# First query and key loads merged, and fourteen more zero products on TensorE, at the start of a cosine-attention and hard-swish kernel

## The chip, the cores and the metric

The kernel runs on one core of a Trainium2 chip. The metric is the device time of one launch in microseconds (us), smaller is better. Each kernel is run several times and the median counts.

## The reference, cut to what matters

Inputs are q, k and v of 8 batches, 12 heads, 448 positions and 64 numbers each, in float32, and two weight matrices of 768x2048 and 2048x768.

```python
q_n = q / (np.linalg.norm(q, axis=-1, keepdims=True) + 1e-06)
k_n = k / (np.linalg.norm(k, axis=-1, keepdims=True) + 1e-06)
scores = np.matmul(q_n, k_n.transpose(0, 1, 3, 2)) / tau
...
attn = np.exp(scores)
attn = attn / (np.sum(attn, axis=-1, keepdims=True) + 1e-09)
...
h = x @ w_in
relu6 = np.clip(h + 3.0, 0.0, 6.0)
g = h * relu6 / 6.0
return (g @ w_out).astype(np.float32)
```

Here x is the attention output with the heads of a position side by side: 3584 rows of 768.

## The kernel before, in words

The whole program is one list of short commands, the table `PLAN` (line 19). A command such as `SQ.2.a.0.7` calls one function with its arguments; each function issues instructions to one or more engines. An engine carries out its own instructions strictly in the order of the list, so the list fixes each engine's order, and semaphores fix who waits for whom. A last letter names the engine: v is DVE (VectorE), a is ACT (ScalarE), p is POOL (GpSimd).

Work goes in 48 pairs of heads (six pairs per batch). Queries and keys are loaded, squared and normalised in items of four heads: item 0 holds queries, item 1 the keys that belong to them, item 2 queries again, and so on through 48 items. An item is a tile of 128 partitions x 2 halves x 448 numbers, 448 KB. The commands around the change are:

- `LQ.j` (line 254): loads item j, one DMA issued by SP. `LQ.0.0` and `LQ.0.1` load the first and the second half of item 0 alone, 224 KB each. `LV` loads values, `W` weights.
- `SQ.j.e.c.n` (line 283): squares n of the item's groups of 64 columns, from c, on engine e. For items 0 and 1 the 14 groups of both halves are counted through, so 0 to 6 are the first half.
- `RE.j` (line 300): DVE sums the squares; `RE.0.0` one half alone.
- `NO.d` (line 318): four small ACT operations (lines 326 to 329) that make the inverse norms of items 2d and 2d+1; `NO.0.0` and `NO.0.1` make those of item 0 and of item 1 alone.
- `NM.j` (line 333): multiplies the item by its inverse norms, on DVE or POOL.
- `TR.j` (line 393): seven TensorE transposes of item j into a PSUM bank; `CQ` (ACT or DVE) and `CK` (DVE) copy queries and keys of a pair of heads from it to SBUF.
- `SC.i.g` (line 474): scores of pair i, group g, on TensorE; `EX.i.g` (line 508): their exponentials on ACT; `VA.i.g` (line 529): the products with the values on TensorE; `FI.i` (line 548): DVE divides by the sums.
- `DP.n` (line 1139): n zero products on TensorE. Each multiplies a 128x128 block of zeros with 248 columns of zeros and writes columns of the PSUM tile PV that nobody reads. Nothing waits for them; they only keep TensorE at work while it would wait.

TensorE's part at the start is, in its order: 23 zero products, the transposes of item 0, 10 zero products, the transposes of item 1, four score products (`SC.0.0`, `SC.0.1`), 3 zero products, two score products (`SC.0.2`), two small ones (`SC.0.3`), the transposes of item 2, the scores of pair 1, 2 zero products, and then the first products with values. A score product of pair 0 goes to one of two PSUM tiles that ACT empties with `EX`, so `SC.0.2` waits for `EX.0.0` and `SC.0.3` for `EX.0.1`.

After the start the list weaves attention, the first matrix product (line 671) and the second one (line 837) together, and TensorE has hardly a pause in them.

Of the kernel before, what the change touches and what calls it, by code (L numbers as in the profile page):

```python
# [16 lines left out]

FIRST = 18
PLAN = [
    "LQ.0.0 LQ.0.1 SQ.0.v.6.2 SQ.0.a.0.6 RE.0.0 SQ.0.a.8.6 RE.0.1 LQ.1.0 SQ.1.p.0.4 SQ.1.a.4.3 RE.1.0 LQ.1.1 SQ.1.v.11.3 SQ.1.a.7.4 RE.1.1 LQ.2 NO.0.0",  # L20
    "SQ.2.a.0.7 LQ.3 NM.0.v.0 NM.0.v.1 NO.0.1 DP.23 TR.0.Z RE.2 LQ.4 LQ.5 NM.1.p.0 NM.1.p.1 SQ.3.a.0.7 RE.3 SQ.5.p.0.7 DP.10 TR.1.Y CQ.0.a CK.0.v",
    "SQ.4.a.0.7 NO.1 CQ.1.a SC.0.0.0 NM.2.p EX.0.0 SC.0.1.1 EX.0.1 RE.4 DP.3 SC.0.2.0 W.0 LV.0 VC.0.p RE.5 CK.1.v SC.0.3.1 EX.0.2 NM.3.v LV.1 EX.0.3 NO.2",
    "VC.2.v W.2 TR.2.Z LQ.7 SC.1.0.0 EX.1.0 SC.1.1.1 EX.1.1 SQ.7.v.0.7 CQ.2.v VC.1.p DP.2 VA.0.0 VA.0.1 VA.0.2 SC.1.2.0 EX.1.2 VC.3.p NM.4.p VA.0.3 FI.0",
    "LQ.8 LQ.6 TR.3.Y CK.2.v SC.1.3.1 DP.1 SC.2.0.0 SQ.6.a.0.7 VA.1.0 VA.1.2 EX.1.3 SC.2.1.1 NM.5.p RE.7 EX.2.0 EX.2.1 CK.3.v VA.1.3 RE.6 SQ.8.p.0.7 VA.1.1",
    "SC.2.2.0 FI.1 EX.2.2 SC.2.3.1 EX.2.3 TR.4.Y VA.2.0 NO.3 LV.2 CQ.3.v SC.3.0.0 CQ.4.v CQ.5.v VC.4.v VA.2.1 VA.2.2 VA.2.3 SC.3.1.1 FI.2 TR.5.Z EX.3.0",
    "EX.3.1 CK.4.v BK.0.Y LV.3 LQ.9 RE.8 SC.3.2.0 SC.3.3.1 VA.3.0 EX.3.2 SC.4.0.0 EX.3.3 EX.4.0 CK.5.v CX.0.v SQ.9.v.0.7 VA.3.2 SC.4.1.1 VA.3.1 SC.4.2.0",
    "VA.3.3 FI.3 BK.2.Z CX.2.v EX.4.1 EX.4.2 NM.6.p TR.6.Y SC.4.3.1 EX.4.3 SC.5.0.0 EX.5.0 VA.4.0 RE.9 W.3 W.1 VA.4.3 SC.5.1.1 VC.6.p VA.4.2 VA.4.1 CQ.7.v",
    "CQ.6.v SC.5.2.0 EX.5.1 EX.5.2 NM.7.p TR.7.Z CK.6.v VC.5.p LQ.10 BK.3.Y CX.3.v SQ.10.p.0.7 SC.5.3.1 CS.7.v EX.5.3 NO.4 BK.1.Y FI.4 DP.3 VA.5.0 CS.6.v",
    "OPEN VA.5.2 SC.6.0 CX.1.v CK.7.v NM.8.p EX.6.0 VA.5.3 VA.5.1 FI.5 SC.6.1 EX.6.1 BK.4 CX.4.v SC.6.2 SC.6.3 EX.6.2 EX.6.3 BK.5 CX.5.v VA.6.0 VA.6.1 TR.8",
    "CQ.8.v CQ.9.v LQ.11 SQ.11.p.0.7 SC.7.0 VA.6.2 EX.7.0 VA.6.3 SC.7.1 SC.7.2 F.0.2 EX.7.1 EX.7.2 RE.11 RE.10 SC.7.3 EX.7.3 FA.0.2 F.0.7 FA.0.7 FI.6",  # L30
    "NM.9.p TR.9 CK.9.v CK.8.v CS.8.v CS.9.v F.0.1 LQ.14 LQ.13 SQ.13.a.0.7 NO.5 F.0.3 FA.0.1 FV.0.7 FV.0.2 FV.0.1 VC.7.p W.5 FA.0.3 LQ.12 LV.4 SQ.12.p.0.7",
    "SC.8.0 SC.8.1 FV.0.3 RE.12 LV.5 W.4 VC.8.p VA.7.0 EX.8.0 EX.8.1 NM.10.p F.0.0 FA.0.0 SC.8.2 VA.7.3 FV.0.0 VA.7.1 VA.7.2 VC.11.p EX.8.2 SC.8.3 EX.8.3",
# [1202 lines left out]
```

## Time and profile before

| | us |
|---|---|
| three timed runs | 399.2, 400.42, 400.69 |
| their median | 400.42 |
| the profiled execution, its own time | 400.38 |
| its span, first to last instruction | 398.5 |

The profile is of one execution. Its page gives the busy time of each engine: PE (TensorE's products), PEld (its weight loads), DVE, ACT, POOL, and SP, which only issues DMAs. A row of the timeline gives the start, the time from the first start to the last end, the engine, the line, the operation, what it writes and reads, and how many instructions were merged; in brackets stands the idle time before it and what ended that. A row of a table by stretches gives the busy time of the engine in the stretch, the number of instructions in brackets, the granted TensorE clock as a share of full speed, the mean share of the 16 DMA engines that was busy, and GB/s. Ends of products on PE are modelled and include their way through the array, so a group of n products takes a little more than n steps.

### The profile page before, as it was taken

Reading aid. Unit: us, or ns where it says so; the run is one execution under the profiler, and the core shown is the slowest. Engines: PE = TensorE matmul, PEld = TensorE weight load, DVE = VectorE, ACT = ScalarE, POOL = GpSimd, SP = SyncE. Lnnn points to the kernel's source line nnn. Section 1 sums busy time; section 2 is a strip of 40 time slices with the busy share of each in tenths; the row PEclk is TensorE's granted clock in tenths of the full one; section 3 lists DMA queues with packets and bytes.
Section 4 is the critical chain, followed back from the end, with each engine's and each line's share of the span. In section 5 each row is a group of like instructions: output and inputs, shape, how many; then the busy total and the mean of one; then the engine's idle time right before and its main releaser. Section 6 shows DMA issues by size and latency. Waiting matters only on the chain.

```text
span 398.5 us, 9978 instructions
## 1 busy us (share of the span) xinstructions
PE 384.1 (96%) x3762; PEld 239.8 (60%) x3762; DVE 309.8 (78%) x545; ACT 295.6 (74%) x670; POOL 297.7 (75%) x269
## 2 busy tenths in 40 slices
PE   5798999999999999999999999999999999999995
PEld 4466556545655556655555555655566679977763
DVE  5898877998969698687766968854878968986862
ACT  5998999989966888896757876897787567744420
POOL 3999885899679947477839694778798988675752
PEclk9799999999999999999999999999999999999999
DMA  7999989997898779896896597666568350012124
GB/s 239 345 237 236 221 214 273 182 160 165 208 211 228 187 179 192 198 228 164 194 213 140 144 203 183 179 157 129 116 127 130 83 122 2 2 40 61 39 61 118
DMA packets 90271, 64.87 MB, mean 163 GB/s; under 512 B 55792, under 2 KB 89456, under 8 KB 90224
## 3 DMA queue, kind: packets, MB, share of 16 engines
q1 hardware_dynamic: 85312, 57.56, 59.4%
q0 software_dynamic: 4512, 6.29, 9.5%
q8 instruction: 29, 0.48, 0.5%
q10 hardware_dynamic: 400, 0.39, 0.3%
q14 instruction: 18, 0.15, 0.1%
HBM read 46.73 MB, written 11.01 MB: 145 GB/s over the span
## 4 chain that ended last, share of the span: by engine, by line
PE 85%; DVE 6%; ACT 3%; DMA 2%; issue 1%; POOL 1%; SPq 0%; DVEq 0%; POOLq 0%; ACTq 0%
PE M L671 18%; PE M L837 16%; PE PV L537 10%; PE V L837 6%; PE M L1026 6%; PE M L502 6%; PE Y L837 4%; PE Z L837 4%; PE Y L671 4%; PE Z L671 3%; PE Y L502 2%; PE Z L502 2%; DMA big<-in_q_dram 1%; DVE on L558 1%; PE Y L1026 1%
## 5 line engine op out<-in xcount | busy, mean ns | idle before, releaser
L521 ACT ACTIVATE att<-M 128x448 bf16<-128x448 f32 x193 | 95.8, 563 | 13.9 <-PE M L502 12.3
L671 PE MATMUL M<-xT,w_in_sb 128*128 128x448 bf16 x396 | 82.9, 353 | 0.0
L671 PEld LDWEIGHTS <-w_in_sb 128*128 128x128 bf16 x576 | 53.1, 98 | 46.8 <-issue 3.4
L341 POOL TENSOR_TENSOR nrm<-big,r 128x896 bf16<-128x896 f32 (+1 forms) x36 | 61.6, 1718 | 17.9 <-ACT r L329 14.5
L537 PEld LDWEIGHTS <-att 128*128 128x128 bf16 (+1 forms) x1536 | 56.4, 97 | 22.7 <-issue 9.9
L537 PE MATMUL PV<-vx,att 128*128 128x65 bf16 (+1 forms) x1536 | 64.9, 194 | 0.1
L837 PEld LDWEIGHTS <-gT 128*128 128x128 bf16 x448 | 42.9, 98 | 28.0 <-POOL gT L812 0.8
L310 DVE TENSOR_REDUCE n<-big 128x14 f32<-128x896 f32 (+1 forms) x50 | 51.6, 1042 | 3.2 <-ACT big L296 2.0
L686 DVE SCALAR_TENSOR_TENSOR gT<-u,M 128x448 bf16<-128x448 bf16 x66 | 39.5, 615 | 18.7 <-ACT u L680 18.4
L680 ACT ACTIVATE u<-M 128x448 bf16<-128x448 f32 x66 | 35.8, 556 | 10.8 <-PE M L671 9.7
L837 PE MATMUL M<-w_out_sb,gT 128*128 128x384 bf16 x224 | 40.4, 326 | 0.0
L298 POOL TENSOR_TENSOR big<-big 128x896 f32<-128x896 f32 (+2 forms) x19 | 31.4, 1655 | 11.7 <-DMA out_dram<-o 3.9
L837 PEld LDWEIGHTS <-gs 128*128 128x128 bf16 x296 | 28.1, 98 | 18.8 <-issue 1.3
L812 POOL TENSOR_TENSOR gT<-gT 128x1024 bf16<-128x1024 bf16 x15 | 31.9, 2123 | 9.5 <-DVE gs L812 9.0
L558 DVE TENSOR_TENSOR on<-PV,rc 128x512 bf16<-128x512 f32 x48 | 33.2, 691 | 1.6
L837 PE MATMUL M<-w_sum,gs 128*128 128x384 bf16 (+1 forms) x192 | 34.0, 323 | 0.0
L502 PE MATMUL M<-tT,kz 64*128 64x448 bf16 (+1 forms) x171 | 33.2, 354 | 0.6 <-DVE gT L686 0.4
L868 POOL TENSOR_TENSOR big<-big 128x384 f32<-128x384 f32 x14 | 18.3, 1304 | 17.8 <-ACT big L625 15.0
L812 POOL TENSOR_TENSOR gs<-gT 128x1024 bf16<-128x1024 bf16 x14 | 29.7, 2123 | 2.4 <-DVE gT L686 1.2
L521 ACT ACTIVATE att<-Z 128x448 bf16<-128x448 f32 x51 | 28.6, 561 | 1.3 <-PE M L502 1.0
L521 ACT ACTIVATE att<-Y 128x448 bf16<-128x448 f32 x50 | 28.1, 563 | 1.2 <-PE Z L502 1.2
L458 POOL COPY km<-tT 64x128 bf16<-64x128 bf16 x34 | 16.3, 481 | 12.6 <-PE Y L502 5.1
(146 smaller groups left out, 755.9 us busy)
## 6 DMA issues: line engine op xcount, KB each, us to landing
big<-in_q_dram SPq DMA_DIRECT2D x23, 448.0 KB, 4.7
big<-in_k_dram SPq DMA_DIRECT2D x23, 448.0 KB, 4.5
out_dram<-o SPq DMA_DIRECT2D x107, 96.0 KB, 2.2
big<-in_v_dram SPq DMA_DIRECT2D x68, 128.0 KB, 3.2
big<-in_v_dram SPq DMA_DIRECT2D x7, 448.0 KB, 7.2
w_out_sb<-in_moe_w_out_dram POOLq DMA_DIRECT2D x4, 768.0 KB, 10.4
w_in_sb<-in_moe_w_in_dram POOLq DMA_DIRECT2D x4, 384.0 KB, 5.8
w_in_sb<-in_moe_w_in_dram POOLq DMA_DIRECT2D x2, 768.0 KB, 7.9
```

The costliest lines, as they stand in the source:

```text
L298: engines[e].tensor_tensor(out=o, in0=i, in1=i, op=ALU.mult)
L310: nc.vector.tensor_reduce(out=n2s[d % 2][:, j % 2, c], in_=sq[:, :, :, :].rearrange("p g c d -> p (g c) d")[:, c, :], axis=AX.X, op=ALU.add,)
L341: engines[e].tensor_tensor(out=nrm[:, :, g, :].rearrange("p c g d -> p g c d"), in0=raw_of[j][:, g, :, :], in1=rs[d % 2][3][:, j % 2, :] . ...
L502: nc.tensor.matmul(o, ks, qt[rows], start=True, stop=True)
L521: nc.scalar.activation(out=o, in_=x, func=AF.Exp, scale=inv_tau)
L537: nc.tensor.matmul(pv_out(j, h), at[rows, n, q_cols(i // HP, j)], vt[rows, 3 + h if name == "M" else 5 * h + int(name[1]), :], start=(name ...
L558: nc.vector.tensor_tensor(out=on[:, :, :, :].rearrange("p j h d -> p h j d"), in0=pv4[:, :, :, 0:D], in1=rc[:, :, :].to_broadcast([128, 2, ...
L671: nc.tensor.matmul(ps[:, 0:S], w_in_sb[:, cc, fc * 128 : (fc + 1) * 128], x[:, cc, 0:S], start=(cc == 0), stop=(cc == CC - 1),)
L680: nc.scalar.activation(out=u[:, :], in_=ps[:, 0:S], func=AF.Relu, bias=0.5, scale=1.0 / 6.0)
L686: nc.vector.scalar_tensor_tensor(out=g[:, fc, c0 : c0 + S], in0=u[:, :], scalar=1.0, in1=ps[:, 0:S], op0=ALU.min, op1=ALU.mult,)
L812: engines[e].tensor_tensor(out=o[:, :, :], in0=x, in1=y, op=op)
L837: nc.tensor.matmul(m, lhs[:, c, :], rhs[:, c, c0 : c0 + width], start=(base is None and c == 0), stop=(c == KC - 1), skip_group_check=True,)
```

## The change

The table `PLAN` alone is changed. The first ten lines of it are broken anew, so the diff looks longer than it is. In its core:

```diff
-"LQ.0.0 LQ.0.1 SQ.0.v.6.2 SQ.0.a.0.6 RE.0.0 SQ.0.a.8.6 RE.0.1 LQ.1.0 SQ.1.p.0.4 SQ.1.a.4.3 RE.1.0 LQ.1.1 SQ.1.v.11.3 SQ.1.a.7.4 RE.1.1 LQ.2 NO.0.0",
+"LQ.0 SQ.0.v.6.2 SQ.0.a.0.6 RE.0.0 SQ.0.a.8.6 RE.0.1 LQ.1 SQ.1.p.0.4 SQ.1.a.4.3 RE.1.0 SQ.1.v.11.3 SQ.1.a.7.4 RE.1.1 LQ.2 NO.0.0 SQ.2.a.0.7 LQ.3",
...
-"... RE.3 SQ.5.p.0.7 DP.10 TR.1.Y CQ.0.a CK.0.v",
+"... RE.3 SQ.5.p.0.7 DP.16 TR.1.Y DP.4 CQ.0.a CK.0.v SQ.4.a.0.7 NO.1",
...
-"... RE.4 DP.3 SC.0.2.0 W.0 LV.0 VC.0.p RE.5 CK.1.v SC.0.3.1 ...",
+"... RE.4 DP.3 SC.0.2.0 DP.4 W.0 LV.0 VC.0.p RE.5 CK.1.v SC.0.3.1 ...",
```

The squares, sums and norms of items 0 and 1 stay cut into halves as they were. What moves is seen best in the order of the instructions on each engine, where + is a row of the changed kernel and - one of the kernel before.

SP's queue, at the very start of the program; `in_q_dram` and `in_k_dram` are the inputs, `big` is the tile that holds the items:

```order
 L1230 UNCONDITIONAL_BRANCH
-L262 DMA big<-in_q_dram 128x448 x2
-L262 DMA big<-in_k_dram 128x448 x2
+L262 DMA big<-in_q_dram 128x2x448
+L262 DMA big<-in_k_dram 128x2x448
 L262 DMA big<-in_q_dram 128x2x448
 L262 DMA big<-in_k_dram 128x2x448
 L262 DMA big<-in_q_dram 128x2x448
 L262 DMA big<-in_k_dram 128x2x448
```

Two whole loads stand in the place of four half ones (x2 is two rows alike), so every later load moves up by two places in SP's queue.

ACT's queue, the squares of items 0 and 1 and the first norms; a DMAHW semaphore tells of the landing of one load:

```order
 L155 ACT_TABLE_LOAD
 L296 ACTIVATE big<-big 128x384 [waits DMAHW0_49]
-L296 ACTIVATE big<-big 128x384 [waits DMAHW1_49]
-L296 ACTIVATE big<-big 128x192 [waits DMAHW2_49]
-L296 ACTIVATE big<-big 128x256 [waits DMAHW3_49]
+L296 ACTIVATE big<-big 128x384
+L296 ACTIVATE big<-big 128x192 [waits DMAHW1_49]
+L296 ACTIVATE big<-big 128x256
 L326 ACTIVATE ln_94<-n_92 128x14 [waits DVE_49]
```

The same four squares stand in the same order; they wait for two landings now and not for four.

TensorE's queue, behind the transposes of item 1 and ahead of the first score product (`nrm` is a normalised item, `xT` here the zeros, `kz` keys, `tT` queries, SC the scores):

```order
 L398 LDWEIGHTS nrm_90
 L398 MATMUL Y<-ident,nrm_90 128x128
+L1142 LDWEIGHTS xT_70
+L1142 MATMUL PV<-xT_70 128x248
...
 L502 LDWEIGHTS kz_80 [waits DVE_49]
 L502 MATMUL SC_135<-tT_84,kz_80 128x448 [waits Activation_49]
```

Four zero products, each a weight load and a product, now stand between the transposes and the first score product, which waits for DVE and ACT as before. In the same way four of them come between `SC.0.2` and `SC.0.3`, and six more join the ten ahead of the transposes of item 1. From there on each engine's order is unchanged.

18 rows, old and new, of the table PLAN are left out of this document.

## The prediction

> **What bounds the kernel now.** I read the table by stretches first, to see where TensorE has room at all.
>
> ```profile
> 0.00:37.00 37.00, 27.88 (x324) 18.53 (x325) 29.73 (x63) 30.04 (x59) 29.15 (x43) 0.91 0.93 260
> 37.00:390.00 353.00, 352.25 (x3419) 219.11 (x3417) 277.87 (x479) 265.60 (x611) 267.37 (x226) 1.00 0.68 154
> ```
>
> From 37 us on TensorE (first column after the length) is busy for 352.25 of 353 us. A microsecond saved before 37 us therefore reaches the end whole, as long as nothing in between has to wait for something that did not move with it; and the change touches nothing behind 17 us. The first 37 us are another world: TensorE is busy for 27.88 us, the granted clock is 0.91 on average, and the DMA engines are at 0.93.
>
> The chain that ended last, followed from the front, says what sets the pace there. It begins with SP's issues, goes over to the load of item 2 until 8.58, and then runs on ACT.
>
> ```profile
> 0.74 0.88 SPq L262 DMA_DIRECT2D big<-in_q_dram  x2
> 1.66 0.91 SPq L262 DMA_DIRECT2D big<-in_k_dram  x2
> 2.61 0.43 SPq L262 DMA_DIRECT2D big<-in_q_dram  x1
> 3.10 0.46 SPq L262 DMA_DIRECT2D big<-in_k_dram  x1
> ...
> 3.38 1.06 ACT L296 ACTIVATE big<-big 128x384 f32<-128x384 f32 x2 [1.36 <-DMA big<-in_q_dram]
> 5.66 0.36 ACT L296 ACTIVATE big<-big 128x192 f32<-128x192 f32 x1 [1.22 <-DMA big<-in_k_dram]
> 6.29 0.42 ACT L296 ACTIVATE big<-big 128x256 f32<-128x256 f32 x1 [0.27 <-DMA big<-in_k_dram]
> ...
> 8.61 0.95 ACT L296 ACTIVATE big<-big 128x896 f32<-128x896 f32 x1 [1.05 <-DMA big<-in_q_dram]
> 9.46 0.20 ACT L326 ACTIVATE ln<-n 128x14 f32<-128x14 f32 x1
> ...
> 10.30 0.93 ACT L296 ACTIVATE big<-big 128x896 f32<-128x896 f32 x1
> 11.14 0.51 ACT L418 COPY tT<-Z 128x448 bf16<-128x448 bf16 x1
> ```
>
> ACT waits 1.05 us for item 2 and starts its square at 8.61. From 8.61 to the first exponential it has no pause, so whatever the landing of item 2 gains is gained for all that follows, up to the next thing that is late.
>
> A second place is TensorE itself between 14.6 and 21.4 us.
>
> ```profile
> 2.51 4.93 PE L1142 MATMUL PV<-xT 128*128 128x248 bf16 x23 [2.51 <-DVE xT L1185]
> 9.09 0.56 PE L398 MATMUL Z<-ident,nrm 128*128 128x128 bf16 x7 [1.64 <-DVE nrm L341]
> 9.49 1.22 PE L1142 MATMUL PV<-xT 128*128 128x248 bf16 x10
> 12.36 0.56 PE L398 MATMUL Y<-ident,nrm 128*128 128x128 bf16 x7 [1.65 <-POOL nrm L341]
> 13.41 0.55 PE L502 MATMUL SC<-tT,kz 64*128 64x448 bf16 x4 [0.49 <-ACT r L329]
> 14.79 0.56 PE L502 MATMUL SC<-tT,kz 64*128 64x448 bf16 x2 [0.40 <-ACT att L521]
> 15.60 0.58 PE L499 MATMUL SC<-tT,kz 64*64 64x448 bf16 x2 [0.25 <-ACT att L521]
> 18.22 1.53 PE L537 MATMUL PV<-vx,att 128*128 128x65 bf16 x24
> 25.55 0.89 PE L537 MATMUL PV<-vx,att 128*128 128x65 bf16 x24
> ```
>
> The same 24 value products took 1.53 us at 18.22 and 0.89 us at 25.55, a ratio of 1.7. A zero product took 4.93/23 = 0.21 us at 2.51 and 1.22/10 = 0.12 us at 9.49. So the array ran slow at the very start (where the profile has no clock record yet and prints 1.00) and again around 18 us. The table by stretches, with PE alone, gives the granted clock:
>
> ```profile
> 7.79:11.21 3.42, 1.62 (x17) 1.00 0.99 348
> 11.21:14.62 3.41, 1.54 (x14) 1.00 1.05 390
> 35.10:38.52 3.42, 2.26 (x43) 1.00 0.97 331
> ...
> 7.79:14.62 6.83, 3.16 (x31) 1.00 1.02 369
> 14.62:21.45 6.83, 6.41 (x60) 0.50 1.11 276
> 21.45:28.28 6.83, 6.28 (x103) 1.00 0.98 294
> 31.69:38.52 6.83, 5.36 (x94) 1.00 1.03 252
> 390.08:396.91 6.83, 3.90 (x25) 1.00 0.59 151
> ```
>
> The clock is 0.50 from 14.62 to 21.45, behind 6.83 us in which PE was busy for 3.16 us (46%). Two engines wait for TensorE in that spell, and neither row would be there at full clock:
>
> ```profile
> 20.28 0.92 ACT L521 ACTIVATE att<-SC 128x896 bf16<-128x896 f32 x1 [0.93 <-PE SC L502]
> ...
> 20.50 0.21 DVE L557 RECIPROCAL rc<-PV 128x8 f32<-128x8 f32 x1 [0.94 <-PE PV L537]
> ```
>
> **The merged loads.** Two issues fall away. SP's issues follow each other every 0.48 us (0.74 to 1.66 for two), and a whole item's issue (0.43 us) costs no more than a half one's (0.44), so item 2 is issued 0.95 us earlier, at 1.66. That is the upper bound of the gain, and it holds only if the DMA engines had nothing to do.
>
> ```profile
> 4.00:5.00 1.00, 0.44 (x1) 1.00 0.73 228
> ```
>
> They mostly had: in their least busy microsecond behind the first loads, 4 to 5 us, their share was 0.73. The bytes ahead of item 2 are the same, in the same order. I count the 0.27 us of idle in that microsecond as what a shorter issue can fill: gain **0.3 us**, bounds 0 and 0.95. I take the value near the low end because it is read where the engines were idle.
>
> The halves have a price. Item 0's first square waits for the whole item: ACT's two squares (3.38 to 4.44) start where DVE's square, which needs both halves, now starts, at 3.99, so 0.6 us later. The wait behind them (1.22 us) takes that. Item 1's squares now wait for the second half's landing, 6.29 in place of 5.66. The sums behind them on DVE slip by that 0.6 us:
>
> ```profile
> 3.99 0.29 DVE L298 TENSOR_TENSOR big<-big 128x128 f32<-128x128 f32 x1 [1.39 <-DMA big<-in_q_dram]
> ...
> 7.34 0.62 DVE L310 TENSOR_REDUCE n<-big 128x7 f32<-128x448 f32 x1
> 7.88 1.15 DVE L341 TENSOR_TENSOR nrm<-big,r 128x448 bf16<-128x448 f32 x2
> ```
>
> The last sum of item 1 then ends at 8.6 and not at 7.96. Its reader is the norm at 9.46, which stands behind item 2's square in ACT's queue, so 0.9 us of cover are there, 0.6 of them left when the square moves up by 0.3. The normalised item 0 comes at 9.6 and its transposes end near 10.2; their copy on ACT is at 11.14, so that is hidden too. If item 2 gained more than 0.9 us, item 1's sum would be late next. Item 3's landing is the other limit:
>
> ```profile
> big<-in_k_dram SPq DMA_DIRECT2D x1, 448.0 KB, 7.0
> ```
>
> It was issued at 3.10 and landed at 10.1, 0.2 us ahead of its square at 10.30. It moves with item 2 or cuts the gain to 0.2. Value: 0.3 us.
>
> **The fourteen zero products.** Six follow the ten. At 0.12 us they end at 9.49 + 16 x 0.12 = 11.4, or at 12.0 if item 0's transposes are 0.6 late; the transposes of item 1 wait for POOL until 12.36. Hidden. Four come after these transposes: from about 12.8 they need 0.5 us at full clock, the pause there is 0.49 us. Hidden, or 0.1 us. The last four stand between `SC.0.2` and `SC.0.3`. The pause is 0.25 us, and a next product can start some 0.16 us ahead of the modelled end (the zeros at 9.49 did, against 9.09 + 0.56 of the transposes before them): at full clock 0.5 us is 0.1 too long at most. At half clock (4 x 0.21 = 0.84) they push `SC.0.3` by 0.4 us.
>
> What they can gain is the clock. With the first ten of them the 6.83 us up to 14.62 hold 3.16 + 10 x 0.12 = 4.4 us of PE (64%), with those last four 4.9 us (71%). The trace has the clock falling after 46% and after 57% (3.90 of 6.83, at the end), and keeping up after 78% (5.36, from 31.69). By the shorter stretches it kept up after 1.62 and 2.26 us of 3.41 and fell after 1.54; the changed ones have 2.3 and 2.0, both above the 1.62 that held once. I take the clock to hold, by the nearest of these rows (1.62).
>
> By the Trainium skill, page "TensorE: Matmul & The Clock Gate", section "HAM oscillation — how this bites in real kernels", the clock only falls after a pause of over about 3.4 us. By that rule it would not have fallen here, and the zeros would be worth nothing. This trace disagrees: the longest pause from 7.79 to 14.62 is the 1.65 us at 12.36, and the clock fell.
>
> If it holds, the gain is the wait that goes: 0.93 us on ACT and 0.94 us on DVE, side by side. It is not the whole of the slow spell, because the values are late next:
>
> ```profile
> 16.69 1.29 POOL L363 CAST vx<-big 64x512 bf16<-64x512 f32 x2
> ...
> 21.80 3.33 POOL L341 TENSOR_TENSOR nrm<-big,r 128x896 bf16<-128x896 f32 x2
> 24.44 0.56 PE L398 MATMUL Y<-ident,nrm 128*128 128x128 bf16 x7
> ```
>
> POOL casts the first values until 17.98, and the value products cannot start much before their 18.22 of now. From there the 24 take 0.89 and not 1.53 us, the scores and the eight small products half their time, and DVE is free at 19.56: the divide comes 0.94 us earlier. POOL itself does not move: item 4's normalised tile is ready at 23.5, and its transposes start at 24.44, so 0.94 us of slack is just used up. Value **0.9 us**, bounds -0.4 (clock falls all the same, the zeros in the way) and 0.94.
>
> **Sum.** Against the profiled execution's 400.38 us: 400.38 - 0.3 - 0.9 = **399.2 us**. The median of the runs, 400.42, is practically the same figure.
>
> **The rivals.** First, the zeros do not hold the clock: it falls at 14.62 as now. For it: 64% lies nearer to the 57% that fell than to the 78% that held. Then `SC.0.3` and all of TensorE behind it, up to the divide at 20.50, come 0.4 us later: 400.38 - 0.3 + 0.4 = 400.5 us. The Trainium skill's rule on pauses, above, gives nothing to the zeros either.
>
> Second, the slow spell comes later, where TensorE is dense. At full clock the stretch from 14.62 holds 6.41/1.7 = 3.8 us of PE, with 0.9 us of work drawn forward 4.7 us, 69%: no safer than the stretch before. If the clock fell at 21.45, the next 6.28 us of PE would take 1.7 times as long, 10.7 us in a stretch of 6.83: 3.9 us more, 400.38 - 1.2 + 3.9 = 403.1 us, slower. It decides if the limit lies above 69% of the stretch. Against it: 1.62 of 3.42 us once held. The Trainium skill, in the same page's section "What's actually happening", has the stretches free-running against the kernel's start; by that a spell can fall elsewhere in some executions, which no row of one trace can show.
>
> Third, the whole of the two issues is gained, the engines being idle by more than the one row shows: 400.38 - 0.95 - 0.94 = 398.5 us. Against it are the share of 0.73 at its lowest, 0.93 over the first 37 us, and a limit of 0.9 us from item 1's sum.
>
> **Chances.** The forecast 0.47, clock falls as before 0.22, spell later 0.11, whole issue gained 0.15, anything else 0.05. About 0.5% (2 us) is what a measurement of this kernel can tell from no change. Below 398.4 lie half of the third rival, a small part of the forecast and of the rest: 0.16. Above 402.4 lie the second rival and part of the rest: 0.13. Between them 0.71. The range goes from 397.8, the third rival less half the spread of before's runs (1.49 us), to 402.0, the first rival with the whole of it; the second rival stays out.
>
> **What would show it.** Right: clock 1.00 from 14.62 to 21.45, no wait of ACT near 20 us for SC, item 2's square at 8.3, the norms at 9.46 still behind it and not behind DVE's sum. Wrong: a 0.50 stretch anywhere between 11 and 37 us, an ACT wait for `n` before the norms, a pause of ACT that ends with `SC.0.3`, or a landing of item 2 that has not moved.

## The result, and the profile after

The changed kernel takes 398.82 us (median of 20 executions, 397.36 to 401.33), the kernel before 400.19 us (20 executions beside them, 399.2 to 402.64). The ratio is 0.9966, with a 95% interval of 0.9953 to 0.998: 0.34% faster. The forecast was 399.2 us, 0.3% faster.

The single profiled execution tells less than usual here. It is the slowest of the twenty (401.33 us, span 399.5), and the reader has to see why before anything is read from it. The granted clock of the changed kernel comes first, from the table by stretches with PE alone:

```profile
5.24:8.66 3.42, 1.20 (x11) 1.00 1.04 387
8.66:12.07 3.41, 2.89 (x18) 0.50 1.06 380
32.55:35.96 3.41, 1.93 (x25) 1.00 0.98 191
35.96:39.38 3.42, 3.39 (x40) 0.50 1.03 361
```

The clock did not hold. It fell at 8.66, behind a stretch in which PE was busy for 1.20 of 3.42 us, and again at 35.96. In the profile before it changed at 7.79, 14.62 and 21.45. By the Trainium skill, page "TensorE: Matmul & The Clock Gate", section "What's actually happening", the clock is judged in stretches of 3.413 us that run freely against the kernel's start. These rows agree: the times at which the clock changes lie whole multiples of 3.41 us apart within a run, and at other places in each run.

What the slow spell at 8.66 costs is read from ACT's rows and from the chain that ended last, which names the zero products (line 1142):

```profile
5.75 0.67 ACT L296 ACTIVATE big<-big 128x192 f32<-128x192 f32 x2 [0.27 <-DMA big<-in_k_dram]
...
7.17 0.93 ACT L296 ACTIVATE big<-big 128x896 f32<-128x896 f32 x1
8.09 0.21 ACT L326 ACTIVATE ln<-n 128x14 f32<-128x14 f32 x1
...
14.10 2.97 ACT L521 ACTIVATE att<-SC 128x896 bf16<-128x896 f32 x4 [1.26 <-PE SC L502]
```

```profile
1.26 4.47 DMA big<-in_k_dram
...
7.44 0.62 DVE n L310
8.06 1.08 DVE nrm L341 x2
9.14 0.05 issue
9.18 0.93 PE Z L398 x7
10.11 2.71 PE PV L1142 x16
12.82 0.41 PE Y L398 x7
```

ACT squares item 2 at 7.17, 1.44 us earlier than before (8.61), and waits for no DMA there. But its first exponential comes at 14.10, later than the 13.82 of before, with a wait of 1.26 us for the first score. The sixteen zero products ahead of item 1's transposes ran mostly at half clock (it was 0.50 until 12.07), 2.71 us of the chain, while item 1 lay ready: POOL had normalised it at 10.96.

```profile
9.12 1.84 POOL L341 TENSOR_TENSOR nrm<-big,r 128x448 bf16<-128x448 f32 x2 [2.70 <-ACT r L329]
```

So this execution shows one thing that came much earlier (the loads) and one that stood in the way (the zeros). Which of them makes the 0.34% cannot be read from it.

### The profile page after: what moved, and what is told of

Its sections match the earlier page's. It is cut to its first block, busy times and chain, and to the rows that moved or that the text cites. A ratio compares the mean times of both kernels' runs of the same rounds, so it can differ in the third digit from the quotient of the medians.

```text
span 399.5 us, 10001 instructions
## 1 busy us (share of the span) xinstructions
PE 385.0 (96%) x3776; PEld 240.9 (60%) x3776; DVE 309.4 (77%) x545; ACT 295.6 (74%) x670; POOL 299.0 (75%) x269
## 3 DMA queue, kind: packets, MB, share of 16 engines
q0 software_dynamic: 4512, 6.29, 9.3%
## 4 chain that ended last, share of the span: by engine, by line
PE 81%; POOL 6%; ACT 3%; DVE 3%; DMA 3%; issue 2%; SPq 0%; POOLq 0%; DVEq 0%; ACTq 0%
PE M L837 16%; PE M L671 16%; PE PV L537 10%; PE V L837 6%; PE M L1026 6%; PE M L502 5%; PE Y L671 4%; PE Y L837 4%; PE Z L837 3%; PE Z L671 3%; DMA big<-in_k_dram 2%; POOL nrm L341 2%; ACT att L521 2%; PE Y L502 2%; PE Z L502 1%
```

## The experiments

Each kernel differs from the one before or the changed one in the table `PLAN` alone and computes the whole result. The theories at the start: BOTH, each half of the change gains about half; LOADS, the merged loads make all of the difference; CLOCK, the zero products do. Kernels of one group ran on one chip beside the kernel before. The ratios are those on record, with their 95% interval; they can differ from the quotient of the two medians by about 0.1%.

### First group: the two halves apart, and more zeros at the start

Loads merged, zero products as before:

```diff
-LQ.0.0 LQ.0.1 ... LQ.1.0 ... LQ.1.1
+LQ.0 ... LQ.1
```

> Only the four half loads are merged into two; the zero products stay 23, 10, 3, 2 and 1 as before. Theory BOTH (the merged loads and the zero products each gain about half): 0.5 to 1.0 us faster than before, median near 399.4 us, executions without a slow clock spell near 398, and slow spells as often as before. Theory LOADS (the loads alone make the difference): the whole 1.4 us, median near 398.8 us. Theory CLOCK (the zero products alone): no change, 400.2 us.

Measured: 397.97 us (median of 12) against 399.65 (29), ratio 0.9958 (0.9945 to 0.9971).

Zero products added, loads in halves:

```diff
-DP.10 TR.1.Y
+DP.16 TR.1.Y DP.4
-SC.0.2.0 W.0
+SC.0.2.0 DP.4 W.0
```

> Only the fourteen zero products are added; the loads stay in halves. Theory BOTH: 0.4 to 0.9 us faster than before, median near 399.5 us, mean granted clock above that of before. Theory LOADS: no change or a little slower, 400.2 to 400.6 us. Theory CLOCK: the whole gain, median near 398.8 us.

Measured: 399.72 us (12), ratio 1.0003 (0.9991 to 1.0016).

The changed kernel again:

> The changed kernel once more, beside the others on the same chip, to have its executions and granted clocks next to theirs. All theories: median near 398.8 us; executions with a granted clock of 1.000 near 397.5 us, those below 0.995 near 400 us.

Measured: 399.21 us (12), ratio 0.9984 (0.9965 to 1.0002).

The changed kernel with a longer first run of zeros:

```diff
-DP.23 TR.0.Z
+DP.35 TR.0.Z
```

> The changed kernel with 35 zero products in place of 23 at the very start, ahead of the first transposes. In its profile PE stood idle for 2.75 us there and the clock fell at 8.66. If slow spells come from that pause (BOTH and CLOCK): fewer executions with a spell, median near 397.8 us, 1 us under the changed kernel, unless the twelve more are still running at half clock when the first transposes could start. If the spells do not matter to the time (LOADS): as the changed kernel, 398.8 us.

Measured: 397.44 us (6), ratio 0.9956 (0.994 to 0.9972).

BOTH and CLOCK fall: the fourteen zero products alone gain nothing, and the merged loads alone gain 0.42%, by the medians more than the whole change did beside them (the two intervals overlap a little). The profile of the repeated changed kernel shows the same rows on PE as the first one, at another place of the clock's stretches:

```profile
9.57 3.29 PE L1142 MATMUL PV<-xT 128*128 128x248 bf16 x16
12.70 0.55 PE L398 MATMUL Y<-ident,nrm 128*128 128x128 bf16 x7
```

Sixteen zeros took 3.29 us. Taking both sets of the changed kernel together, 15 of 32 executions had a mean granted clock of 0.997 or more, and their median is 397.5 us; that of the other 17 is 399.3. For the kernel before the same cut (over the 82 executions that ran beside the three groups) gives 399.7 (13 executions) and 400.1 (69): there the two parts lie much closer together.

### Second group: which zeros, and what of the merging

By now theory STREAM (only the loads gain, and the pause ahead of the first transposes decides on the slow spells) stood against ZEROS (the fourteen are needed once the loads are early).

Merged loads, 35 zeros at the start, none of the fourteen:

```diff
-DP.23 TR.0.Z
+DP.35 TR.0.Z
```

> Merged loads and 35 zero products in place of 23 at the very start, but none of the change's fourteen. Theory STREAM (the merged loads give the whole gain, the fourteen zero products nothing, and the pause before the first transposes decides on slow clock spells): median near 397.4 us, as the changed kernel with 35. Theory ZEROS (the fourteen are needed once the loads are early): 398 us or more.

Measured: 397.65 us (9) against 400.39 (29), ratio 0.9941 (0.992 to 0.9962).

The changed kernel without the six:

```diff
-DP.16 TR.1.Y DP.4
+DP.10 TR.1.Y DP.4
```

> The changed kernel with ten zero products again ahead of item 1's transposes, so that only the eight others of the fourteen stay. Theory STREAM, with the six in the way whenever the clock is low (16 at half clock took 2.9 us): near the loads alone, 398.0 us, and executions with a clock below 0.996 at most 1.2 us above the best, not 3 us. Theory ZEROS: slower than the changed kernel by 0.3 us or more.

Measured: 398.18 us (9), ratio 0.9946 (0.9926 to 0.9966). Three of the nine had a clock below 0.997; they lay 0.9 to 2.7 us above the best, so the limit of 1.2 us that was expected did not hold. The profiled one (400.06) had its slow spell at 35.67, far behind these zeros. The medians lean the way of STREAM (the changed kernel's ratios were 0.9966 and 0.9984), but the intervals overlap, so that the six cost anything in the median is not shown.

Item 0 in halves, item 1 merged, zeros as before:

```diff
-LQ.0 SQ.0
+LQ.0.0 LQ.0.1 SQ.0
```

> Zero products as before, item 1 merged, item 0 in halves: one issue more than with both merged. Theory STREAM in the form that the DMA engines start on too little work (a half item first) and then run uneven: item 2 lands near 8 us and most of the gain is lost, 399.2 to 399.7 us. In the form that each issue costs its 0.48 us: half of the gain is left, near 398.8 us.

Measured: 400.13 us (12), ratio 0.9997 (0.998 to 1.0014), slower than either form had allowed.

Items 0 and 1 merged, items 2 and 3 in halves:

```diff
-LQ.2 ... LQ.3
+LQ.2.0 LQ.2.1 ... LQ.3.0 LQ.3.1
```

> Zero products as before, items 0 and 1 merged, items 2 and 3 in halves: as many issues as in the kernel before, but the halves come later. Form TOO LITTLE WORK FIRST: item 2 lands near 7 us and the gain stays, 398.0 us. Form HALVES ARE SLOW (a half transfer itself runs badly wherever it stands): items 2 and 3 land late by 1 us or more, 399 us or above.

Measured: 400.34 us (12), ratio 1.0001 (0.9985 to 1.0017).

STREAM stands in its main point: without the fourteen zeros, and with the first pause filled, the kernel is as fast as with them. One half load at the head of the queue takes the whole gain away, though item 1 stays merged. The DMA traffic shows it, from 2 to 9 us (last column GB/s, the one before it the share of the DMA engines; the busy time in these rows is ACT's). The kernel before, and the one with zeros alone, both with half loads first:

```profile
2.00:9.00 7.00, 2.99 (x10) 1.00 0.92 282
```

```profile
2.00:9.00 7.00, 3.06 (x10) 1.00 0.91 294
```

Item 0 alone in halves:

```profile
4.00:5.00 1.00, 0.48 (x1) 1.00 0.84 247
...
2.00:9.00 7.00, 3.46 (x11) 1.00 0.95 324
```

The changed kernel, both merged, and the one with items 2 and 3 in halves:

```profile
4.00:5.00 1.00, 0.45 (x2) 1.00 1.04 401
...
2.00:9.00 7.00, 4.02 (x15) 0.98 1.00 360
```

```profile
2.00:9.00 7.00, 3.99 (x15) 1.00 0.98 357
```

With a whole item first the engines move 354 to 360 GB/s (all ten such profiles, those of the third group included). With a half first they move 282 to 324 (four profiles). Half loads of items 2 and 3 do not disturb the traffic.

The slow spells can be kept out of this comparison. The kernel with item 0 in halves and the one with items 2 and 3 in halves have the same zero products, and in their profiles the clock was 0.50 at nearly the same time, from 9.92 to 13.33 and from 9.80 to 13.21. Their first exponentials, in that order:

```profile
14.47 2.97 ACT L521 ACTIVATE att<-SC 128x896 bf16<-128x896 f32 x4 [0.88 <-PE SC L502]
```

```profile
13.14 2.97 ACT L521 ACTIVATE att<-SC 128x896 bf16<-128x896 f32 x4 [0.64 <-PE SC L502]
```

Their first divides come at 20.57 and 18.67 us (20.50 before). With the clock alike, the half item at the head costs 1.3 us at the first exponential and 1.9 us at the first divide.

The mean traffic is not the whole of it. In the four profiles that start with a half, item 2's square starts at 8.0 to 8.9 us. In seven of the ten that start with a whole item it starts at 6.8 to 7.3, but in the other three at 8.5 to 8.6, though the traffic there was 354 to 357 GB/s. The profile of the merged loads alone, the slowest of its twelve executions, is one of these three:

```profile
8.58 0.95 ACT L296 ACTIVATE big<-big 128x896 f32<-128x896 f32 x1 [1.61 <-DMA big<-in_q_dram]
```

Its clock fell and rose within 0.12 us of the times of before (at 14.50 and 21.33), and its first divide came only 0.03 us ahead of before's: with item 2 late, the merged loads gained nothing at the start. So the gain comes with the early landing of item 2, and the mean traffic alone does not tell it. Why item 2 was late in three profiles, and how often it is in executions that were not profiled, is not known.

Yet the kernel with items 2 and 3 in halves gained nothing in its median; its profile shows where. Its instructions run 1.5 us ahead of before until 338 us, and lose it at one place at the end, where POOL and DVE each add halves of activations (line 1009). First that kernel, DVE and POOL, then the same two rows of the kernel before:

```profile
338.97 1.56 DVE L1009 TENSOR_TENSOR xT<-xT 128x672 bf16<-128x672 bf16 x1
```

```profile
338.71 1.45 POOL L1009 TENSOR_TENSOR att<-xT 128x672 bf16<-128x672 bf16 x1
```

```profile
340.09 0.50 DVE L1009 TENSOR_TENSOR xT<-xT 128x672 bf16<-128x672 bf16 x1
```

```profile
340.18 1.73 POOL L1009 TENSOR_TENSOR att<-xT 128x672 bf16<-128x672 bf16 x1
```

Before, DVE's addition starts 0.09 us ahead of POOL's and takes 0.50 us. Here POOL's starts first, and DVE's takes 1.56 us and ends 0.37 us after POOL's; TensorE waits behind it (0.96 us at 342.25).

### Third group: what is left

Item 0 merged, item 1 in halves:

```diff
-LQ.1 SQ.1.p.0.4 SQ.1.a.4.3 RE.1.0
+LQ.1.0 SQ.1.p.0.4 SQ.1.a.4.3 RE.1.0 LQ.1.1
```

> Zero products as before, item 0 merged, item 1 in halves: one issue more than with both merged, like the kernel with item 0 in halves, but the DMA engines start on a whole item. Theory STREAM, form TOO LITTLE WORK FIRST: the stream is even from 2.6 us on, item 2 lands near 7 us (8.5 if one engine falls behind), and the gain stays, 397.5 to 398.5 us. Form HALVES ARE SLOW: 399.5 us or above, as with item 0 in halves.

Measured: 398.04 us (7) against 400.19 (24), ratio 0.9941 (0.9919 to 0.9962). Its traffic from 2 to 9 us is 356 GB/s. The kernel with item 0 in halves issues the same three transfers for items 0 and 1, a whole one and two halves, in another order. So the number of issues does not decide; what stands at the head of the queue does. Whether it acts by its size or in some other way was not tried.

The kernel before with 35 zeros at the start:

```diff
-DP.23 TR.0.Z
+DP.35 TR.0.Z
```

> The kernel before, loads in halves, with 35 zero products in place of 23 at the very start and nothing else. It tells the price of the slow clock spell under late loads. If the term of 0.9 us for a held clock is right: clock 1.00 from 14.6 to 21.4 us, no wait of ACT for the third score group of pair 1, and 0.9 us faster, median near 399.3 us beside 400.2. If the late loads hide the clock: no change.

Measured: 399.84 us (12), ratio 0.9986 (0.9969 to 1.0004). In its profile the clock was 1.00 from 7.89 on, and from 36 us on it ran 0.6 to 0.8 us ahead of before. But only 5 of its 12 executions reached a clock of 0.997. Item 0's transposes start at 10.24 us in its profile, and the pause ahead of them is still 1.25 us long; whether that is the reason is not shown. The median's change is not told apart from none.

The best of the pieces together:

```diff
-DP.23 TR.0.Z
+DP.35 TR.0.Z
-DP.16 TR.1.Y DP.4
+DP.10 TR.1.Y DP.4
```

> The changed kernel with 35 zero products at the start and ten ahead of item 1's transposes (the two fours stay). All theories: 397.4 us, with at most a quarter of the executions above 398.5; better than the changed kernel by 1 us or more.

Measured: 397.35 us (7), ratio 0.9934 (0.991 to 0.9957): 0.66% faster than the kernel before. The changed kernel did not run beside it, and its interval (0.9953 to 0.998) just touches this one, so the 1 us or more that was expected against it is likely but not shown. In its profile PE is free when POOL hands over item 1, and ACT does not wait:

```profile
6.97 0.93 ACT L296 ACTIVATE big<-big 128x896 f32<-128x896 f32 x1
...
12.27 2.54 ACT L521 ACTIVATE att<-SC 128x896 bf16<-128x896 f32 x3
```

```profile
9.38 1.22 PE L1142 MATMUL PV<-xT 128*128 128x248 bf16 x10
10.81 0.56 PE L398 MATMUL Y<-ident,nrm 128*128 128x128 bf16 x7 [0.20 <-POOL nrm L341]
```

The exponentials start at 12.27 in place of 13.82: 1.55 us. Of the 22 executions of the three kernels with merged loads and 35 zeros, 18 had a clock of 0.997 or more (median 397.4 us).

Items 2 and 3 in halves, the same kernel as before:

> Items 0 and 1 merged, items 2 and 3 in halves, once more, since its first profile kept a gain of 1.5 us until 338 us and lost 1.4 us there at once (a POOL addition started just ahead of a DVE one and DVE's took 1.56 in place of 0.50 us). If that was a chance of one execution: median near 398 us. If it comes back: 400.3 us again, and the same two rows.

Measured: 399.99 us (12), ratio 0.9998 (0.998 to 1.0015). It came back, with the same two rows (DVE's addition ends 0.36 us after POOL's here):

```profile
339.37 1.54 DVE L1009 TENSOR_TENSOR xT<-xT 128x672 bf16<-128x672 bf16 x1
```

```profile
339.09 1.46 POOL L1009 TENSOR_TENSOR att<-xT 128x672 bf16<-128x672 bf16 x1
```

In both profiles of this kernel POOL starts first, in all the others DVE does, by a tenth of a microsecond. Why half loads at the start turn the order of two instructions at 339 us was not found out, and no kernel was run that changes this order alone: that it takes the gain in all 24 executions is inferred from two profiles.

## Why the prediction was right, and where it was not

The time and the sign were right, the reasons for them only in part. Two terms were wrong in opposite directions, by about a microsecond or more each, so that the sum came out near the measured time was luck. By the prediction's own signs, the changed kernel's profile shows the clock at 1.00 from 14.62 to 21.45, no wait of ACT for SC near 20 us and an earlier item 2, which spoke for it, but also a 0.50 stretch between 11 and 37 us, which spoke against it.

**The merged loads, 0.3 us: mis-sized.** The direction and the place were right; the loads alone gained 1.7 us (399.65 to 397.97), above the bound of 0.95 us that came from the two issues. The step that failed: "I count the 0.27 us of idle in that microsecond as what a shorter issue can fill". The idle microsecond from 4 to 5 us was not a gap that an earlier issue fills but one mark of traffic that ran uneven until 9 us, 282 GB/s where 360 were to be had. The busy share hides most of this: from 2 to 9 us it is 0.92 against 1.00, 8% less, while the traffic is 22% less. What made it uneven was the half transfer at the head of the queue, not the number of issues: with item 1 in halves the issues are one more than in the changed kernel and the gain stays, with item 0 in halves it is gone. How a half at the head does this stays open.

The cover for the halves was right, though item 0 came later than counted (ACT's first square at 4.55 and not 3.99). The last sum of item 1 and item 2's square now end together: in the changed kernel DVE's sum ends at 8.06 and the norm starts at 8.09, behind the square of 7.17 to 8.10. That the sum "would be late next" is what happened, only later in gain: 1.4 us and not 0.9, since item 1 landed at 5.73 and not at 6.29.

**The zero products, 0.9 us: the step "I take the clock to hold" failed.** The clock fell in both profiles of the changed kernel and was below 0.997 in 17 of 32 executions. The sum of PE's work was made for the stretches as they lay in the one profile of before. They lie elsewhere in each execution, and the weakest place is the pause ahead of item 0's transposes (2.75 us in the changed kernel's profile), which none of the fourteen fills; it was 1.64 us before. With the twelve extra zeros that fill part of it (0.64 to 1.00 us were left in the three profiles with merged loads) 18 of 22 executions held the clock.

The size of the term was right for an execution in which the clock holds. The profile with merged loads, 35 zeros and none of the fourteen happened to have item 2 landing as late as before (issued at 1.75, the last column is the time to landing):

```profile
big<-in_q_dram SPq DMA_DIRECT2D x1, 448.0 KB, 6.8
```

```profile
14.62:21.45 6.83, 5.44 (x79) 1.00 0.97 245
```

```profile
19.33 0.20 DVE L557 RECIPROCAL rc<-PV 128x8 f32<-128x8 f32 x1
```

With the first exponential at 13.81, as before, and the clock at 1.00, the divide comes at 19.33 and not at 20.50, and from 36 us on everything runs 0.9 us ahead. The wait of 0.94 us was the price, as counted.

"Hidden" for the six was wrong at half clock. Only the last four had been priced there (0.4 us). In a slow spell sixteen took 2.9 to 3.3 us, and with item 1 ready at 10.96 in the changed kernel's profile they held its transposes up to 12.66. The kernel with zeros alone shows the two sides of them in one execution. Its clock was 0.50 from 10.25 to 13.66, and ACT waited for the first score:

```profile
14.63 1.73 ACT L521 ACTIVATE att<-SC 128x896 bf16<-128x896 f32 x2 [0.89 <-PE SC L502]
```

That is 0.81 us later than before (13.82). But the clock was up again from 13.66, the wait near 20 us did not come, and from there on the execution ran 0.2 us ahead: what the zeros cost in one spell they gained by the next. Beside merged loads the zeros can stand in the way longer, since item 1 is ready 1.3 us earlier there (10.96 against 12.23).

**The rivals.** The first (the zeros do not hold the clock) happened, at another price. The second (a later spell) happened in some executions, at 35.96 in the changed kernel's profile: there its lead over before of 0.7 us turned into a lag of 0.7 us, 1.4 us in place of the 3.9 that were worked out for the denser stretch. The third (the whole issue gained) was too small.

**The sum.** 0.3 + 0.9 = 1.2 us was forecast and 1.4 us measured; what is behind it is 1.7 us for the loads, less what the zeros give back by the medians (0.3 us between the two sessions' gains, 1.2 us between the two kernels side by side). The intervals overlap, so this second part is not shown clear of the spread. With the loads in halves the fourteen zeros gain at most 0.1% (ratio 0.9991 at the low end).

## What to carry to other kernels

Put keep-alive work where the longest pause is (here twelve zeros there went with a held clock, fourteen elsewhere did not), and count it at the slow clock too: work that is hidden at full speed stands in the way when the clock has already fallen. Try a stream of loads with a full transfer at its head, and ask of a dip in DMA traffic what comes before it, rather than count it as room to fill. One profile is one draw where the clock's stretches run freely: compare the granted clock of many executions before explaining a microsecond.

## What the runs showed of the hardware that had not been expected

- Starting SP's stream of loads with a transfer of 224 KB left the DMA engines at 282 to 324 GB/s from 2 to 9 us, starting it with 448 KB at 354 to 360; the kernels with item 0 and with item 1 in halves issue the same three transfers in another order (324 against 356).
- The clock fell behind a stretch of 3.41 us in which PE was busy for 1.93 us (32.55 to 35.96), while it had held behind 1.62 us in the profile before. Busy time alone does not decide it; what else counts was not tried.
- A DVE addition of 128x672 took 0.50 us where it started 0.09 us ahead of a POOL addition of the same size, and 1.54 to 1.56 us where POOL started 0.26 to 0.28 us ahead; there it ended 0.36 to 0.37 us after POOL's.
- With the same DMAs at the head of SP's queue, item 2 landed in time for a square at 6.9 to 7.2 us in four profiles (the changed kernel twice, with 35 zeros, and the last kernel) and at 8.5 to 8.6 in three.
